# Later first loads, and 16 warming instructions moved ahead, in a recurrence followed by an MLP

## The chip, the cores and the metric

The kernel runs on one core of one Trainium2 chip. The metric is the device time of one execution in microseconds. Engines are named as in the profile: PE (TensorE matmuls), PEld (its weight loads), DVE (VectorE), ACT (ScalarE), POOL (GpSimd), SP (SyncE, which here only issues transfers).

## The reference

The first part is a linear recurrence with a decay for every channel; its output, with the heads side by side, goes through a two-layer MLP with an exact Gelu.

```python
# r, k, v, w: (4, 8, 768, 48) float32; u: (8, 48)
for t in range(S):
    kt, vt, rt, wt = (k[:, :, t], v[:, :, t], r[:, :, t], w[:, :, t])
    cur = np.einsum('bhd,bhe->bhde', u[None] * kt, vt)
    y[:, :, t] = np.einsum('bhd,bhde->bhe', rt, state + cur)
    state = wt[:, :, :, None] * state + np.einsum('bhd,bhe->bhde', kt, vt)
...
x = attn_out.transpose(0, 2, 1, 3).reshape(B * S, H * D)   # 3072 x 384
h = x @ w_in                                               # 384 x 2048
g = 0.5 * h * (1.0 + erf(h * inv_sqrt2))
return g @ w_out                                           # 2048 x 384
```

`w_in` and `w_out` come as float64; the kernel turns them into float32 on the chip.

## The kernel before, in words

The work is cut into eight tiles, x = 0 to 7: a half sequence (T = 384 steps) of one batch element with all eight heads. A tile's recurrence is done in chunks of C = 64 steps. Inside a chunk the decays are gathered by doubling: there are six levels, h = 1, 2, 4, 8, 16, 32. At each level PE makes products of k and r for all chunks (`products`, the matmuls of line 575), DVE copies the part that belongs to this level into `a_sb` under a mask (line 639; at h = 16 and 32 ACT does it, line 636), and DVE multiplies r and k by the decay products of blocks of length h (lines 617 and 628). The level's update needs the level's products to be done, since it overwrites what they read, and the next level's products need the update. At h = 1 there is a second product, the diagonal with u.

The first tile (x = 0) is done in two units of two head pairs each, so that one unit's PE work can lie beside the other's DVE work. After the levels come the transposes of k (line 798), k times v (line 824), the chunk's own y (line 865), the chain of states on DVE (lines 839 and 844), and the states' part of y (line 894). The result is copied to `xT`; the rows of the fourth head pair go there through six small transfers (`pack`, line 886), three issued by SP and three by ACT.

The MLP of tile 0 (`first_mlp`) runs beside the recurrence of tile 1. Its first layer makes one group of 128 hidden units after another (line 1084, three matmuls of the program each, six in the records), in two PSUM banks in turn; the Gelu of line 1086 frees a bank. Later tiles use `mlp`, which lies beside the next tile's recurrence in the same way.

Order on every engine is the order in which the program writes instructions. For each tile a string in `PLAN` sets it: each letter takes the next piece from a stream. In the first tile's string `.` and `s` are the two units, `f` the next tile's recurrence (its first steps), `l` the loads, `c` and `p` the conversion of weights, `w` the next tile's v, and `x` warming matmuls. What is left of the streams after the string is written out behind it.

The transfers around the change are all issued by SP, in order:

- `load_first` (line 274) loads r, k and w of the first tile, in six parts, and behind it `load_v(0, nc.sync)` (line 278) loads v. Neither waits for anything.
- `weight_in(i, True)` (lines 326 and 327) loads the i-th piece of w_in in three thirds of 256 KB. Ahead of each third, DVE writes one element of the destination; the transfer has to wait for that, so the place of the letter `l` in DVE's order paces the transfer.
- `load_second` (lines 285 and 286) loads r, k and w of the second tile in eight shares of 288 KB, paced in the same way.
- Pieces 3 and up come from `conversion` without a mark (line 322).

A piece of weights is converted by three ACT instructions (`prepare`, lines 459, 460 and 462) and two DVE instructions (`finish`, lines 471 and 475). Piece 0 is prepared by the first `c`, piece 1 by the first `p`, piece 2 by the second `p`.

Warming matmuls multiply zeros into a bank that nobody reads (`keep_warm`, line 349). There are 12 of 128 columns at the start, followed by two long ones (line 353); two of 512 columns behind certain `products` of the first tile; and two times three of 512 columns where the string has `x`. On PE each is one weight load and one matmul.

Of the kernel before, what the change touches and what calls it, by code (L numbers as in the profile page):

```python
# [10 lines left out]
F32 = mybir.dt.float32  # L11
# [10 lines left out]
C = 64  # L22
# [10 lines left out]
BANK = 512  # L33
# [3 lines left out]
NC_SP = 8  # L37
HALFWAY = 2
PLAN = {
    0: "l.s....llsl.lssslslss.lc.l.slslls...ssss..lcs.s.s.l.ss..ss..sccs.c.s.llpssslw..cs.ffpccxx",  # L40
    1: (
        "swcs.clc.cs.wccscwcc.csccsw..cwlsccccccsc.cs.swcccc.ccc.s.cwlssccsclcs.cwss.lscccsw.c.cwcw"
        ".s..clw..lw..wwccc..cccc.scc.l.cslfccscfccw.fcffy.w.y..fw....ywyw..yyxxx.wyfxx..x.w..y.fyx"
# [149 lines left out]
def kernel(  # L193
# [9 lines left out]
    nc = tc.nc  # L203
# [12 lines left out]
    io = ctx.enter_context(tc.tile_pool(name="io", bufs=2))  # L216
# [8 lines left out]
    def pair(name):  # L225
        return pools["d"].tile([128, 2, BANK], F32, name=name, tag="d")
# [23 lines left out]
    loaded = {}  # L250

    def units_of(x):
        return NPART if x == 0 else 1
# [4 lines left out]
    bufs = [io.tile([128, 3 * NP * T], F32, name=f"rkw{i}", bufs=1) for i in range(2)]  # L258
# [7 lines left out]
    def load_first():  # L266

        t = bufs[0]
        loaded[0] = [None, None]
        size = 3 * NP * T // units_of(0)  # L270
        nc.scalar.dma_start(out=u_sb, in_=u)
        for i, part in ((0, 2), (0, 0), (0, 1), (1, 0), (1, 1), (1, 2)):
            s = slice(i * size + part * size // 3, i * size + (part + 1) * size // 3)
            nc.sync.dma_start(out=t[:, s], in_=rkw[0, :, s])

    def load_v(x, dma):
        loaded[x][1] = io.tile([128, v.shape[2]], F32, name="v_in", bufs=1)
        dma.dma_start(out=loaded[x][1], in_=v[x])
# [35 lines left out]
    def weight_in(i, gate=False):  # L314

        if i < len(pieces):
            dst, src = pieces[i]
            raws[i] = cv.tile([128, PIECE], I64, name="raw", bufs=AHEAD) if wide else None
            if wide:
                dst = raws[i].rearrange("p (a c) -> p a c", a=dst.shape[1])  # L320
            if not gate:
                nc.sync.dma_start(out=dst, in_=src)
                return
            for a in range(dst.shape[1]):
                if wide:
                    nc.vector.memset(dst[:, a].bitcast(U32)[:, 0:1], 0)
                nc.sync.dma_start(out=dst[:, a], in_=src[:, a])
                yield

    load_first()  # L330
    load_v(0, nc.sync)


    zeros = const.tile([128, BANK], BF16, name="zeros")
# [8 lines left out]
    def keep_warm(n, elsewhere=False, n_cols=BANK):  # L343
        if elsewhere:
            t = pair("warm")[:, 0]
        else:
            t = bank("warm")
        for _ in range(n):
            nc.tensor.matmul(t[:, 0:n_cols], lhsT=zeros[:, 0:128], rhs=zeros[:, 0:n_cols], start=True, stop=True)

    keep_warm(12, n_cols=BANK // 4)
    for _ in range(2):
        nc.tensor.matmul(bank("warm"), lhsT=zeros[:, 0:2 * 128].bitcast(F32), rhs=long_zeros, start=True, stop=True)

# [39 lines left out]
    for i, h in enumerate(QUARTERS[:1]):  # L394
        for a in range(3):
            w_q = (3 - a) * C // 4
            z = q_ints[1 if a == 0 else 2]
# [81 lines left out]
    def attention(x, unit):  # L479
# [3 lines left out]
        np_ = len(parts)  # L483
# [6 lines left out]
        rc, kc = (z.rearrange("p (b i c t) -> p b i c t", b=np_, c=2, t=C) for z in (r, k))  # L490
# [77 lines left out]
        def products(bs, right, width, warm=True):  # L568
            d = pair("d")
            n = 0  # L570
            for b in bs:
                for i in range(NI):
                    for g in range(2):
                        for p in range(2):
                            nc.tensor.matmul(d[half[p], g, n * width:(n + 1) * width],  # L575
                                             lhsT=kc[half[g], b, i, p], rhs=right(half[g], b, i, p),
                                             start=True, stop=True)
                    n += 1
            if x == 0 and warm:
                keep_warm(2)  # L580
            return d[:, :, 0:n * width]
# [10 lines left out]
        def halves():  # L592

            for h in LEVELS:
                m = C // 2 // h
                if np_ < NPART:

                    d = products(range(np_), lambda z, b, i, p: rc[z, b, i, p], C, 1 < h < 8)
                    d = d.rearrange("p g (n m two j) -> p g n m two j", two=2, j=h, m=m)[:, :, :, :, 1, :]
                else:  # L600
                    right = rc.rearrange("p b i c (m two j) -> p b i c m two j", two=2, j=h)[:, :, :, :, :, 1, :]
                    d = products(range(np_), lambda z, b, i, p: right[z, b, i, p], C // 2)
                    d = d.rearrange("p g (n m j) -> p g n m j", j=h, m=m)
                if h == 1:
                    yield
                    diag = diagonal()
                yield

                r2 = r.rearrange("p (n two j) -> p n two j", two=2, j=h)[:, :, 1, :]
                t2 = tot[h].rearrange("p (n two) -> p n two", two=2)[:, :, 0:1].to_broadcast(r2.shape)  # L610
                k2 = k.rearrange("p (n two j) -> p n two j", two=2, j=h)[:, :, 0, :]
                tk = tot[h].rearrange("p (n two) -> p n two", two=2)[:, :, 1:2].to_broadcast(k2.shape)
                rk = bass.AP(tensor=r2.tensor, offset=r2.offset, ap=[r2.ap[0], [n_u - h, 2]] + list(r2.ap[1:]))
                tt = bass.AP(tensor=t2.tensor, offset=t2.offset, ap=[t2.ap[0], [1, 2]] + list(t2.ap[1:]))

                def update(z, r2=r2, t2=t2, k2=k2, tk=tk):
                    nc.vector.tensor_mul(*((k2, k2, tk) if z is k else (r2, r2, t2)))

                if x == 0 and m == 1:

                    update(k)
                    last_r.append(lambda: update(r))
                elif x == 0 and h == 1:
                    update(r)
                    yield
                    update(k)
                else:
                    nc.vector.tensor_mul(rk, rk, tt)
                yield
                ah = at.rearrange("p g n (m two j) -> p g n m two j", two=2, j=h)[:, :, :, :, 1, :]  # L630
                if h >= 16:

                    for p in range(2):
                        for i in range(m):
                            s = slice(p * 64 + i * 2 * h, p * 64 + i * 2 * h + h)
                            nc.scalar.copy(out=ah[s, :, :, i], in_=d[s, :, :, i])
                else:
                    mask = masks[h].rearrange("p (m j) -> p m j", j=h).unsqueeze(1).unsqueeze(1)
                    nc.vector.copy_predicated(out=ah, mask=mask.to_broadcast(ah.shape), data=d)
                if h == 1:  # L640
                    copy_diagonal(diag)
                yield
# [267 lines left out]
        else:  # L910
# [8 lines left out]
            for turn in range(2):  # L919
                for i in range(NI):  # L920
                    for b in range(np_):
                        p = (b + turn) % 2
# [10 lines left out]
            for turn in range(2):  # L933
                ysb = ysb_of() if turn == 0 else ysb
                a = ys[turn][1][:, :, 0:NI * C].rearrange("p b (q i t) -> p b q i t", q=Q, t=C)
                for z in range(2):
                    s = slice(z * G, z * G + D)
# [9 lines left out]
        if split:  # L947
            for c, copy in enumerate((nc.scalar.copy, nc.vector.tensor_copy)):
                for z in range(2):
                    s = slice(z * G, z * G + D)  # L950
                    copy(out=xT[s, 0:Q, :].rearrange("p q (i c t) -> p (q i) c t", c=2, t=C)[:, :, c, :],
                         in_=ys[0][0][c][s, 0:NI * C].rearrange("p (i t) -> p i t", t=C))
# [3 lines left out]
        for b in reversed(range(np_)):  # L956
            for q in reversed(range(Q)):
# [5 lines left out]
                if which < NJ:  # L963
                    for z in range(2):
                        s = slice(z * G, z * G + D)
# [274 lines left out]
    second = load_second(nc.sync)  # L1240
# [13 lines left out]
    def next_v():  # L1254
        load_v(1, nc.sync)
        yield

    def warm():
        for _ in range(2):
            keep_warm(3, True)  # L1260
            yield

    def masks_and_sums():
# [6 lines left out]
    for x in range(NX):  # L1270
        following = attention(x + 1, 0) if x + 1 < NX else iter(())
        if x == 0:
            streams = {
                ".": units[0], "s": units[1], "f": following, "c": pieces_of_w, "w": next_v(), "x": warm(),
                "p": prepare_apart(),
                "l": chain(weight_in(0, True), islice(second, 5), weight_in(1, True), second, weight_in(2, True)),
            }
        else:
            streams = {
                **(mlp(x - 1) if x > 1 else {".": first_mlp()}),  # L1280
                "s": slots, "f": following,
                "l": load(x + 1, nc.sync),
                "x": sums_of_x(x),
                "w": masks_and_sums() if x == 1 else chain(h_sums([1]), o_sums(EARLY, len(FORMS_O))) if x == 2 else iter(()),
                "y": o_sums(0, EARLY) if x == 1 else iter(()),
                "c": pieces_of_w if x == 1 else iter(()),
            }
        for c in PLAN[x]:
            next(streams[c], None)
        for c in ".slxwp" if x == 0 else ".slxwcy" if x == 1 else ".vgeoslxw":  # L1290
            while next(streams[c], streams) is not streams:
                pass
        slots = following
        if x == 1:
            fewer_pairs()
# [63 lines left out]
```

## Time and profile before

| | |
|---|---|
| median of 3 runs | 576.1 us (575.36 to 579.16) |
| profiled execution, its own time | 577.52 us |
| its span, first to last instruction | 575.7 us |
| PE busy | 551.3 us (96%) |
| PEld busy | 491.1 us (85%) |
| DVE busy | 489.2 us (85%) |
| ACT busy | 334.1 us (58%) |
| POOL busy | 106.1 us (18%) |
| granted TensorE clock, mean | 1.00 |

A row in order of time gives the start and the length in us, the engine, the line, the operation, what it writes and reads, how many, and in brackets the idle time before it and what ended that; "issue" stands for a wait that the profile doesn't show. SPq and ACTq are the issuing of transfers. A row of stretches gives the stretch, its length, the busy time of PE, PEld, DVE, ACT and POOL with the number of instructions, the granted clock, the busy share of the 16 DMA engines and GB/s. A row of transfers gives destination and source, the issuing engine, how many, KB each, and the time from issue to landing. Tile names are the program's: `rkw` holds r, k and w, `d` the products, `raw` a weight piece as it is loaded, `v_in` is v.

### The profile page before, as it was taken

The page shows a single profiled execution, that of the slowest core. Times are in us where ns is not written, and L with a number is a line of the kernel's source. Part 1 is how long each engine was busy: PE and PEld are TensorE (multiplying, and loading weights), DVE is VectorE, ACT ScalarE, POOL GpSimd, SP SyncE. Part 2 cuts the span into 40 slices and gives each one's busy share as a digit, 9 for nine tenths or more (in the row PEclk, how much of TensorE's full clock was granted, in tenths as well). Part 3 has the DMA queues.
Part 4 walks back from the last instruction along what each step waited for, and adds up shares of the span by engine and source line. Part 5 has one row for each costly group of instructions (what it writes and reads, how often), then busy time and mean ns, then how long its engine had stood idle before and what let it go on. Part 6 is the DMA issues. An engine that isn't in the chain of part 4 may idle for free. (4 is left out here: it accounts for less than half of the span.)

```text
span 575.7 us, 17712 instructions
## 1 busy us (share of the span) xinstructions
PE 551.3 (96%) x7412; PEld 491.1 (85%) x7420; DVE 489.2 (85%) x977; ACT 334.1 (58%) x768; POOL 106.1 (18%) x105
## 2 busy tenths in 40 slices
PE   7689999999998999999999999999999999999997
PEld 4576665689998989999898998989898988999997
DVE  7889879999989989798989979799888989755464
ACT  2468995347753677347763477527772478535820
POOL 5100000016200460006400252005500072000000
PEclk9999999999999999999999999999999999999999
DMA  8559742239342782558623593337915384200001
GB/s 303 178 159 370 239 142 87 81 86 154 47 82 64 175 106 36 139 156 131 81 46 114 135 165 44 60 91 159 131 30 135 84 105 62 43 25 30 0 1 41
DMA packets 71646, 62.15 MB, mean 108 GB/s; under 512 B 32912, under 2 KB 56720, under 8 KB 71568
## 3 DMA queue, kind: packets, MB, share of 16 engines
q1 hardware_dynamic: 50112, 45.62, 26.4%
q0 software_dynamic: 21216, 15.34, 20.3%
q8 instruction: 58, 0.95, 0.7%
q14 instruction: 20, 0.16, 0.1%
q10 hardware_dynamic: 240, 0.08, 0.1%
HBM read 36.24 MB, written 4.72 MB: 71 GB/s over the span
## 5 line engine op out<-in xcount | busy, mean ns | idle before, releaser
L1148 POOL DMA_DIRECT2D g<-o_sb x78 | 94.9, 1490 | 370.7 <-ACT g L1117 347.2
L1197 DVE TENSOR_TENSOR g<-g 128x512 f32<-128x512 f32 x112 | 75.1, 688 | 24.3 <-PE o_ps L1073 21.3
L1117 ACT COPY o_sb<-u_ps 128x384 f32<-128x384 f32 (+1 forms) x56 | 25.8, 461 | 67.6 <-PE u_ps L1073 66.2
L1073 PE MATMUL h_ps<-forms_x,w_in_sb 128*128 128x192 f32 x280 | 57.7, 332 | 0.0
L1073 PE MATMUL o_ps<-w_out_sb,g 128*128 128x192 f32 x280 | 50.5, 327 | 0.5 <-DVE g L1197 0.5
L1117 ACT COPY g<-h_ps 128x384 f32<-128x384 f32 x84 | 40.4, 482 | 16.3 <-PE h_ps L1073 14.4
L1073 PEld LDWEIGHTS h_ps<-forms_x,w_in_sb 128*128 128x128 f32 x280 | 46.6, 190 | 2.7 <-ACT g L1117 2.2
L1073 PEld LDWEIGHTS o_ps<-w_out_sb,g 128*128 128x128 f32 x280 | 46.0, 190 | 1.2 <-DVE g L1197 0.8
L1166 ACT ACTIVATE g<-g 128x384 f32<-128x384 f32 x98 | 46.2, 519 | 0.3
L1073 PE MATMUL o_ps<-t,g 128*128 128x192 f32 x224 | 41.4, 328 | 0.1
L726 ACT COPY a_sb<-d 32x320 f32<-32x320 f32 (+5 forms) x108 | 39.3, 364 | 3.6 <-DVE a_sb L784 1.7
L1073 PEld LDWEIGHTS o_ps<-t,g 128*128 128x128 f32 x224 | 36.8, 190 | 0.7 <-PE u_ps L1073 0.3
L1073 PE MATMUL h_ps<-forms_x,s 128*128 128x192 f32 x168 | 35.5, 334 | 0.0
L1073 PE MATMUL h_ps<-xT,w_in_sb 128*128 128x192 f32 x168 | 35.0, 331 | 0.1
L710 PE MATMUL d<-kx,rkw 64*64 64x96 f32 x1152 | 32.0, 248 | 3.0 <-ACT a_sb L726 1.9
L710 PEld LDWEIGHTS d<-kx,rkw 64*64 64x64 f32 x1152 | 25.6, 133 | 9.6 <-issue 4.3
L1084 PE MATMUL h_ps<-xT,w_in_sb 128*128 128x384 f32 x96 | 33.0, 494 | 0.2
L1073 PE MATMUL u_ps<-xT,w_in_sb 128*128 128x192 f32 x168 | 32.5, 328 | 0.1
L1073 PE MATMUL u_ps<-w_out_sb,g 128*128 128x192 f32 x168 | 30.9, 332 | 1.4 <-ACT o_sb L1115 0.8
L1092 PE MATMUL o_ps<-w_out_sb,g 128*128 128x384 f32 x96 | 31.7, 489 | 0.0
L575 PEld LDWEIGHTS d<-rkw 64*64 64x64 f32 x1152 | 19.1, 134 | 14.2 <-issue 8.5
L739 DVE COPY_PREDICATED a_sb<-quarter,d 128x480 f32<-128x480 uint8 (+5 forms) x54 | 23.2, 440 | 8.7 <-PE d L710 7.4
(178 smaller groups left out, 1206.2 us busy)
## 6 DMA issues: line engine op xcount, KB each, us to landing
g<-o_sb POOLq DMA_DIRECT2D x78, 192.0 KB, 4.2
rkw<-in_rkw_dram SPq DMA_DIRECT2D x54, 256.0 KB, 3.7
raw<-in_w_out_dram SPq DMA_DIRECT2D x8, 768.0 KB, 5.4
v_in<-in_v_dram SPq DMA_DIRECT2D x8, 584.0 KB, 4.6
out_dram<-o_sb SPq DMA_DIRECT2D x24, 192.0 KB, 2.1
raw<-in_w_in_dram SPq DMA_DIRECT2D x5, 768.0 KB, 9.2
rkw<-kx SPq DMA_DIRECT2D x72, 48.0 KB, 2.1
rkw<-in_rkw_dram SPq DMA_DIRECT2D x6, 384.0 KB, 6.8
```

The costliest lines, as they stand in the source:

```text
L575: nc.tensor.matmul(d[half[p], g, n * width:(n + 1) * width], lhsT=kc[half[g], b, i, p], rhs=right(half[g], b, i, p), start=True, stop=True)
L710: nc.tensor.matmul(d[half[p], g, i * 3 * C // 2:(i + 1) * 3 * C // 2], lhsT=kc[half[g], n // NI, n % NI, p], rhs=rx[half[g], 2 * n + p], s ...
L726: nc.scalar.copy(out=at[z, g, first:behind, (a + 1) * h:], in_=d[z, :, :, to] if g == slice(None) else d[z, :, to])
L739: nc.vector.copy_predicated(out=an[:, :, :, :, (a + 1) * h:], mask=mask.to_broadcast(data.shape), data=data)
L1073: nc.tensor.matmul(o, lhsT=lhsT, rhs=rhs, start=start, stop=True, skip_group_check=True)
L1084: nc.tensor.matmul(h_ps, lhsT=w_in_sb[:, f // FI, j, f % FI * 128:(f % FI + 1) * 128], rhs=xT[:, j, :], start=(j == 0), stop=(j == NJ - 1))
L1092: nc.tensor.matmul(o, lhsT=gs[f // FG][:, f % FG, i * 128:(i + 1) * 128], rhs=w_out_sb[:, f, :], start=(f == 0), stop=(f == NF - 1))
L1117: nc.scalar.copy(out=o, in_=z)
L1148: nc.gpsimd.dma_start(out=o, in_=saved[q, t], accum_op=ALU.add)
L1166: nc.scalar.activation(out=o, in_=z, func=AF.Gelu, scale=MINUS.get(h, 1.0))
L1197: nc.vector.tensor_add(o, o, g_block(what[3:5]))
```

## The change

The order of the first tile's steps other than loads stays the same letter by letter; the `l` letters move, and there are two more of them. Four things are edited:

- v of the first tile is no longer loaded right behind r, k and w. It comes in two halves with marks, as part of the `l` stream, behind the first piece of w_in.
- Every `l` stands later in the string. With the `l` steps written out (`w0` to `w2` the thirds of pieces 0 to 2, `v` the halves of v, `t` the shares of the second tile), the start of the string reads `w0 . s .... w0 w0 s t . t sss t s t ss . t c . w1 . s w1 s w1 t s` before, and `. s .... w0 s . w0 sss w0 s v ss . v c . t . s t ss . t .. t sss t s .. w1` after. Its end reads `w2 w2 p sss w2 w .. c s . ff p cc xx` before, and `t p sss w2 w .. w2 c s . w2 ff p cc xx` after. The `p` ahead of `sss` prepares piece 1, the last one piece 2. The SP part of `pack` is in the third of these `s`.
- The matmuls of the levels h = 2 and h = 4 of both units of the first tile are no longer followed by two warming matmuls each, 8 in all. At the start there are 20 short warming matmuls instead of 12.
- The six warming matmuls at the string's end have 64 columns instead of 512.

```diff
 PLAN = {
-    0: "l.s....llsl.lssslslss.lc.l.slslls...ssss..lcs.s.s.l.ss..ss..sccs.c.s.llpssslw..cs.ffpccxx",
+    0: ".s....ls.lssslslss.lc.l.slss.l..lsssls..lcs.s.sl..lss.l.ss..sccs.lc.s.lpssslw..lcs.lffpccxx",
...
+    def first_v():
+        loaded[0][1] = t = io.tile([128, v.shape[2]], F32, name="v_in", bufs=1)
+        for i in range(2):
+            s = slice(i * v.shape[2] // 2, (i + 1) * v.shape[2] // 2)
+            nc.vector.memset(t[:, s.start:s.start + 1], 0.0)
+            nc.sync.dma_start(out=t[:, s], in_=v[0][:, s])
+            yield
+
     load_first()
-    load_v(0, nc.sync)
...
-    keep_warm(12, n_cols=BANK // 4)
+    keep_warm(20, n_cols=BANK // 4)
...
-                    d = products(range(np_), lambda z, b, i, p: rc[z, b, i, p], C, 1 < h < 8)
+                    d = products(range(np_), lambda z, b, i, p: rc[z, b, i, p], C, False)
...
     def warm():
         for _ in range(2):
-            keep_warm(3, True)
+            keep_warm(3, True, 64)
             yield
...
-                "l": chain(weight_in(0, True), islice(second, 5), weight_in(1, True), second, weight_in(2, True)),
+                "l": chain(weight_in(0, True), first_v(), islice(second, 5), weight_in(1, True), second, weight_in(2, True)),
```

## The prediction

> **What bounds the kernel now.** I read the page first, then the table by stretches, then the order of time of the first 50 us, where the whole edit lies.
>
> ```profile
> span 575.7 us, 17712 instructions
> PE 551.3 (96%) x7412; PEld 491.1 (85%) x7420; DVE 489.2 (85%) x977; ACT 334.1 (58%) x768; POOL 106.1 (18%) x105
> q8 instruction: 58, 0.95, 0.7%
> ```
>
> PE is busy for 96% of the span. The third row is PE's own instructions: 14832 matmuls and weight loads in 58 transfers, so one transfer for every 256 instructions.
>
> ```profile
> 10.00:15.00 5.00, 3.69 (x165) 2.81 (x161) 4.93 (x10) 0.73 (x1) 4.07 (x9) 1.00 0.98 339
> 15.00:20.00 5.00, 3.24 (x127) 2.35 (x121) 4.02 (x10) 2.21 (x3) 2.05 (x3) 1.00 0.70 212
> 40.00:45.00 5.00, 5.00 (x108) 3.41 (x106) 4.83 (x11) 4.82 (x7) 0.00 (x0) 1.00 0.86 263
> 45.00:50.00 5.00, 5.00 (x108) 3.26 (x106) 4.95 (x7) 4.12 (x7) 0.00 (x0) 1.00 1.02 377
> ```
>
> The columns are the length, then PE, PEld, DVE, ACT and POOL busy, the granted clock, the DMA share and GB/s. In the first loop DVE is the fuller engine (4.93 and 4.02 of 5 us against 3.69 and 3.24 of PE). From 40 us on PE has no gap, so whatever the first loop gains or loses at its end is carried to the end of the kernel nearly whole; a wait put into PE at 45 us is carried in the same way.
>
> ```profile
> 13.19 0.80 PE L575 MATMUL d<-rkw 64*64 64x64 f32 x38 [0.24 <-issue]
> 14.46 0.93 PE L575 MATMUL d<-rkw 64*64 64x64 f32 x48
> 15.32 0.39 PE L349 MATMUL warm<-zeros 128*128 128x512 bf16 x1
> 15.86 0.67 PEld L575 LDWEIGHTS d<-rkw 64*64 64x64 f32 x38 [0.42 <-issue]
> 18.12 0.45 PE L575 MATMUL d<-rkw 64*64 64x64 f32 x11 [1.46 <-issue]
> 18.66 0.96 DVE L628 TENSOR_TENSOR rkw<-rkw,tot_sb 128x768 f32<-128x768 f32 x1 [0.45 <-issue]
> 20.03 0.96 DVE L628 TENSOR_TENSOR rkw<-rkw,tot_sb 128x768 f32<-128x768 f32 x1 [0.41 <-PE d L575]
> 22.68 1.39 PE L575 MATMUL d<-rkw 64*64 64x64 f32 x80 [0.61 <-issue]
> 23.43 0.96 DVE L628 TENSOR_TENSOR rkw<-rkw,tot_sb 128x768 f32<-128x768 f32 x1 [0.15 <-PE d L575]
> 26.41 1.49 PEld L575 LDWEIGHTS d<-rkw 64*64 64x64 f32 x95 [0.49 <-issue]
> 27.45 1.20 DVE L617 TENSOR_TENSOR rkw<-rkw,tot_sb 128x384 f32<-128x384 f32 x2 [0.84 <-issue]
> 33.98 0.86 PE L865 MATMUL y_ps<-a_sb,v_in 64*64 64x64 f32 x44 [1.39 <-issue]
> 37.71 1.59 PE L575 MATMUL d<-rkw 64*64 64x32 f32 x94 [0.57 <-issue]
> ```
>
> PE stops in the middle of a burst several times with nothing that releases it. Between the restarts at 13.19 and 18.12 lie 38 pairs of load and matmul, two warming pairs, 48 pairs, two warming pairs and 38 pairs: 128 pairs, 256 instructions. These stops are waits for the next block of instructions, and DVE's idle times at 18.66, 20.03, 23.43 and 27.45 follow bursts that were late through them: 0.45 + 0.41 + 0.15 + 0.84 = 1.85 us. [...]
>
> **The change part by part.** *Eight more short warming matmuls ahead.*
>
> ```profile
> 1.19 1.46 PE L349 MATMUL warm<-zeros 128*128 128x128 bf16 x12 [1.19 <-DVE two L338]
> 2.44 3.73 PE L353 MATMUL warm<-zeros 128*128 128x512 f32 x4
> 6.93 0.93 PE L575 MATMUL d<-rkw 64*64 64x64 f32 x48 [0.76 <-DMA rkw<-in_rkw_dram]
> ```
>
> One costs 1.46 / 12 = 0.12 us, eight cost 0.98. PE waits 0.76 us for the load of k there, so 0.22 us at most comes out the other side, and DVE's first update waits for that burst. Without the cover it would be the whole 0.98.
>
> *Two warming matmuls after each of the second and third levels' four bursts left out.* That is 8 matmuls and 8 weight loads, 16 instructions, the number put in ahead; from the end of the third level every later block boundary falls where it did. In between it falls 16 and then fewer instructions earlier, 16 x 0.93 / 96 = 0.16 us of a burst. A pair costs PE 0.42 us (the idle time of the weight load behind it at 15.86). The four pairs make 1.7 us of PE, but DVE is the fuller engine, so the gain can only come out of its 1.85 us of idle time. A burst that begins 0.42 earlier asks for its next block earlier, and the block itself comes with less traffic around it. The lower bound is no gain, the upper 1.85. The 0.45 and the 0.41 are removed if the third level's bursts move up by the warming pair and half the stop; of the 0.84, 0.49 is a block's wait. I take 1.4 for these, less 0.2 for the start: 1.2 gained. What is late next is DVE itself, which then runs without a gap.
>
> *Six warming matmuls at the loop's end get 64 columns instead of 512.*
>
> ```profile
> 39.24 1.47 PE L349 MATMUL warm<-zeros 128*128 128x512 bf16 x5
> 40.63 1.87 PEld L575 LDWEIGHTS d<-kx,rkw 64*64 64x64 f32 x96 [0.42 <-ACT kx L524]
> ```
>
> The burst behind them waits for ACT's product with u. Nothing is gained; PE now idles there instead.
>
> *The first loads paced.* The first piece of w_in and v are held back by marks that DVE writes between its own operations.
>
> ```profile
> 14.27 0.96 ACT L459 ACTIVATE f<-raw 128x768 f32<-128x768 f32 x1 [4.70 <-DMA raw<-in_w_in_dram]
> 24.18 2.58 ACT L636 COPY a_sb<-d 16x192 f32<-16x192 f32 x8 [6.94 <-PE d L575]
> 29.89 1.03 PE L824 MATMUL kv_ps<-v_in,kx 64*64 64x48 f32 x48 [0.23 <-ACT kx L800]
> ```
>
> ACT idles 6.94 us behind the first piece's conversion, and v, now issued near 15 us, is first read at 29.89. Both delays cost nothing. The marks are 0.06 us of DVE each, one more than before. SP waits at each mark; behind it stand only later loads, and the last mark before the three xT transfers is passed near 31 us, long before these are due.
>
> *The third piece of w_in.* Here the pacing bites. Its three thirds go out one by one; now two leave SP before the xT transfers and one behind them, and after the change all three come behind, with the next tile's v between the first and the second.
>
> ```profile
> 31.20 1.68 SPq L327 DMA_DIRECT2D raw<-in_w_in_dram  x2
> 36.60 1.86 SPq L886 DMA_DIRECT2D xT<-ysb  x3
> 38.57 0.56 SPq L327 DMA_DIRECT2D raw<-in_w_in_dram  x1
> 39.23 1.23 SPq L278 DMA_DIRECT2D v_in<-in_v_dram  x1
> 40.51 0.43 SPq L322 DMA_DIRECT2D raw<-in_w_in_dram  x1
> 42.17 0.93 ACT L459 ACTIVATE f<-raw 128x768 f32<-128x768 f32 x1 [0.15 <-DMA raw<-in_w_in_dram]
> 42.58 6.07 PE L1084 MATMUL h_ps<-xT,w_in_sb 128*128 128x384 f32 x18
> 42.99 1.01 ACT L460 ACTIVATE e<-raw,two 128x768 f32<-128x768 uint32 x1
> 44.03 1.10 ACT L462 ACTIVATE e<-raw 128x768 f16<-128x768 f32 x1
> 45.15 0.49 ACT L1086 ACTIVATE g<-h_ps 128x384 f32<-128x384 f32 x1
> ```
>
> ```profile
> raw<-in_w_in_dram SPq DMA_DIRECT2D x1, 256.0 KB, 3.5
> v_in<-in_v_dram SPq DMA_DIRECT2D x1, 584.0 KB, 5.7
> ```
>
> ACT already waits 0.15 us for this piece now: the third issued at 38.57 takes 3.5. After the change one third takes that place, v follows, and the last two are issued near 40.5 and 41. Ahead of the last byte stand 3 x 256 + 584 KB = 1.38 MB. At 263 GB/s from 40 to 45 us (1.32 MB) and 377 behind that, they are through at 45.2. If v lands as now, at 39.23 + 5.7 = 44.9, the 0.52 MB behind it add 1.4 at 377 GB/s: 46.3, and a little more if pieces behind share. Bounds: 42.17 (no loss, if the rings interleave them ahead of v) and 46.8; I take 46.0, near the end that the v row gives. ACT's conversion then starts 3.83 us later. Behind it in ACT's order stand L460, L462 and the first Gelu; behind that Gelu waits PE, since the first layer has two banks: its third group of six matmuls reuses the bank that the Gelu frees. That group is due at 42.58 + 2/3 x 6.07 = 46.63 and the Gelu now ends at 45.64, a cover of 0.99. PE is stopped 3.83 - 0.99 = 2.84 us; without the cover it would be 3.83. DVE's shift of the same piece waits too, but less than PE. What SP holds behind these thirds is 0.52 MB later, 1.4 us, and is converted behind the late piece anyway.
>
> **The sum.** -1.2 + 2.84 = +1.6 us. The profiled execution took 577.52 us (575.7 of span and 1.8 around it), 1.4 above the median of the runs, 576.1. The changed kernel comes to 579.1 in a like execution and 577.7 in the median. With the bounds: -1.85 (574.3) to +0.22 + 4.63 - 0.99 = +3.9 (580.0); that is the likeliest case's own range.
>
> **The rivals.** *(a) The late piece stays hidden.* Its thirds land by 43 because SP gets through its queue earlier than I count, or the rings let them pass v. For it: the loop itself ends earlier and SP's issues with it. Against it: v's 5.7 us to landing. Then only the gain stands: 576.1 - 1.2 = 574.9.
>
> *(b) The clock falls; slower.* Place: PE's stop ahead of the third group at 46 us, and the second and third levels, where PE was busy 3.24 of 5 us with four of the warming pairs and has less now. Price: at the start the 128-column matmuls take 0.12 us, while 512 columns at 39.24 take 1.47 / 5 = 0.29 or less, so a slow PE is about half as fast, and it stayed so for about 5 us (1.19 to 6.17). Where PE has no gap, 5 us at half speed lose 2.5. In the levels five bursts of 0.93 double, 4.7 us, of which about half hides behind DVE. 577.7 + 2.5 + 2.5 = 582.7. [...]
>
> *(c) The fetch stops vanish.* With light traffic each block comes in time and the bursts close up: 0.24 + 1.46 + 0.61 + 0.49 + 1.39 + 0.57 = 4.8 us of stops and 4 x 0.42 = 1.7 of warming, 6.4 in all: 569.7. Against it: DVE is idle only 1.85 us around them, and the stops at 33.98 and 37.71 lie where the traffic is light already.
>
> *(d) No gain and the latest landing:* 580.0, or a little over it if the pieces behind come late as well.
>
> **How the numbers follow.** The forecast has 0.45, (a) 0.17, (b) 0.24, (c) 0.10, (d) 0.04. One per cent, about what a measurement of this kernel can tell from no change, is 5.8 us: below 570.3 or above 581.9. Faster comes from (c), 0.10; slower from (b) and half of (d), 0.26; the rest, 0.64, is within 1%. The range leaves (c) out below and the upper half of (b) above: 573.8 to 583.0.
>
> **What would show it.** Right: ACT's L459 near 42 to 45 us with several us of idle time that a transfer of raw ended; PE idle ahead of the L1084 matmuls, released by ACT's L1086; DVE's idle times near 18.7 and 20.0 gone; the burst that starts at 36.84 now about 1.2 us earlier; L617's first update up to 0.2 later. Wrong: the conversion without a wait, a granted clock under 1.00 after 10 us, the 1.46 us stop still whole, or a time that moves by over 4 us with the first 50 us as described, which would put the cause behind the first loop.

## The result, and the profile after

The changed kernel took 586.6 us in the median (584.34 to 587.91, six runs) against 578.7 for the kernel before (575.36 to 581.92, six runs beside it): a ratio of 1.0139, 95% interval 1.0096 to 1.0182. It is slower by 1.4%. The forecast was 577.7 with 573.8 to 583.0, 1.6 us more than before; measured were 7.9 us more, so it was wrong. The profiled execution took 586.21 us; before's took 577.52.

The head of the page after:

```profile
span 584.4 us, 17722 instructions
PE 553.5 (95%) x7417; PEld 494.6 (85%) x7420; DVE 490.0 (84%) x979; ACT 333.2 (57%) x768; POOL 106.1 (18%) x105
PEclk9887999999999999999999999999999999999999
```

The span grew by 8.7 us and the engines' sums hardly moved. The last row is the granted clock in 40 slices of 14.6 us: it is below full in slices 2 to 4, so what is lost lies in the first 60 us. The table by stretches of the kernel after (columns as before) says where:

```profile
10.00:15.00 5.00, 3.37 (x176) 2.72 (x167) 4.97 (x9) 0.00 (x0) 4.09 (x9) 1.00 0.46 151
15.00:20.00 5.00, 2.93 (x144) 2.69 (x144) 5.00 (x11) 2.88 (x3) 1.89 (x3) 0.92 0.72 213
30.00:35.00 5.00, 1.88 (x127) 1.74 (x120) 4.34 (x26) 3.25 (x4) 0.00 (x0) 1.00 0.82 262
35.00:40.00 5.00, 4.57 (x140) 4.57 (x143) 1.27 (x5) 0.48 (x1) 0.00 (x0) 0.66 0.03 9
50.00:55.00 5.00, 2.08 (x5) 1.05 (x5) 4.39 (x6) 4.91 (x7) 0.00 (x0) 0.84 1.03 375
```

From 10 to 15 us the loads are thinner (151 GB/s, 339 before), and DVE is full, as foretold. Then PE is busy for only 1.88 us between 30 and 35 and for 2.08 between 50 and 55 (before: 3.61 and 5.00), and with or behind each of these holes stands a granted clock below 1 (0.66 from 35 to 40 us, 0.84 from 50 to 55).

The order of time after, at the places of those holes. First the end of the first loop:

```profile
26.43 0.56 DVE L624 TENSOR_TENSOR rkw<-rkw,tot_sb 128x384 f32<-128x384 f32 x1 [0.66 <-issue]
28.87 0.55 PE L831 MATMUL kv_ps<-v_in,kx 64*64 64x48 f32 x18 [0.23 <-ACT kx L807]
30.18 0.33 SPq L286 DMA_DIRECT2D rkw<-in_rkw_dram  x1
35.43 0.86 PE L872 MATMUL y_ps<-a_sb,v_in 64*64 64x64 f32 x44 [3.55 <-issue]
36.18 3.79 PE L901 MATMUL y_ps<-rkw,st 64*64 64x64 f32 x77
38.45 0.48 ACT L977 COPY ysb<-y_ps 128x384 f32<-128x384 f32 x1 [5.16 <-PE y_ps L901]
```

and the rows of the kernel before for the same steps that the prediction did not show:

```profile
34.73 2.32 PE L894 MATMUL y_ps<-rkw,st 64*64 64x64 f32 x79
36.10 0.48 ACT L970 COPY ysb<-y_ps 128x384 f32<-128x384 f32 x1 [1.79 <-PE y_ps L894]
48.58 1.60 PE L575 MATMUL d<-rkw 64*64 64x32 f32 x96
```

The y burst (44 matmuls of line 872) stops for 3.55 us with nothing that releases it; before the same stop took 1.39. The rows of transfers further down have a packet of the instruction queue (q8) 2.3 us ahead of the restart, at 33.10; the stop is taken from that to be a wait for a block of instructions. The 77 matmuls behind it take 3.79 us, where 79 took 2.32.

Then the MLP's first groups, after:

```profile
40.93 1.31 SPq L327 DMA_DIRECT2D raw<-in_w_in_dram  x1
42.34 0.38 SPq L278 DMA_DIRECT2D v_in<-in_v_dram  x1
42.81 0.86 SPq L327 DMA_DIRECT2D raw<-in_w_in_dram  x2
42.92 2.70 PE L582 MATMUL d<-kx,rkw 64*64 64x64 f32 x96 [1.23 <-ACT kx L531]
45.55 4.61 PE L1091 MATMUL h_ps<-xT,w_in_sb 128*128 128x384 f32 x12
49.64 0.89 ACT L466 ACTIVATE f<-raw 128x768 f32<-128x768 f32 x1 [5.25 <-DMA raw<-in_w_in_dram]
53.09 3.90 PE L1091 MATMUL h_ps<-xT,w_in_sb 128*128 128x384 f32 x6 [2.92 <-ACT g L1093]
56.91 1.60 PE L582 MATMUL d<-rkw 64*64 64x32 f32 x96
```

This is the chain that the prediction drew: two thirds behind v, ACT waiting 5.25 us for `raw`, the Gelu late, PE stopped 2.92 us ahead of the third group. But the six matmuls of that group take 3.90 us, where a group took about 2.0 before (6.07 / 3).

The loss as a running difference, after minus before, at the start of the same event:

| event | before | after | difference |
|---|---|---|---|
| k times v | 29.89 | 28.87 | -1.02 |
| y burst again at work | 33.98 | 35.43 | +1.45 |
| copy of the result (`ysb`) | 36.10 | 38.45 | +2.35 |
| first MLP group | 42.58 | 45.55 | +2.97 |
| third group (before: 42.58 + 2/3 x 6.07) | 46.63 | 53.09 | +6.46 |
| next level's products | 48.58 | 56.91 | +8.33 |
| span | 575.7 | 584.4 | +8.7 |

So the wait for blocks costs 2.47 (2.16 by the longer stop in the y burst, the rest by one of 0.37 in k times v that before did not have), the third piece's stop 2.92, and slower matmuls most of the rest: 0.90 up to the copy, 0.62 up to the first group, 6.46 - 2.97 - 2.92 = 0.57 in the first two groups, and 1.87 in the third. The granted clock of the kernel after is 0.50 in four stretches of 3.41 us each, from 19.24, 36.31, 43.13 and 53.38 us. A table of stretches of 3.4 us shows that the slower matmuls lie where the clock is low:

```profile
32.90:36.30 3.40, 0.87 (x51) 0.87 (x52) 1.91 (x11) 0.39 (x1) 0.00 (x0) 1.00 0.42 156
36.30:39.70 3.40, 3.40 (x78) 3.40 (x75) 0.97 (x5) 0.48 (x1) 0.00 (x0) 0.50 0.02 5
39.70:43.10 3.40, 2.17 (x123) 2.01 (x123) 3.25 (x7) 1.80 (x4) 0.00 (x0) 1.00 0.27 58
43.10:46.50 3.40, 3.40 (x98) 2.98 (x95) 3.26 (x10) 1.28 (x3) 0.00 (x0) 0.51 0.93 320
50.00:53.40 3.40, 0.48 (x2) 0.30 (x2) 2.79 (x3) 3.34 (x5) 0.00 (x0) 1.00 1.05 402
53.40:56.80 3.40, 3.40 (x6) 1.35 (x4) 3.36 (x7) 2.69 (x4) 0.00 (x0) 0.50 0.99 351
```

In these stretches the clock is either 1.00 or 0.50, give or take the rounding of the stretch. Each of the three at half clock follows one that PE did not fill (0.87 us, 2.17, 0.48).

When the late block arrived can be read from the transfers. In the kernel after, between 33.0 and 33.2 us (packets, MB, share of the engines):

```profile
q1 hardware_dynamic: 38, 0.07, 93.5%
q8 instruction: 1, 0.02, 29.8%
```

in the kernel before, between 31.3 and 31.7:

```profile
q8 instruction: 1, 0.02, 18.0%
q1 hardware_dynamic: 10, 0.01, 7.4%
```

Before, the block came some 1.5 us behind the start of k times v, with the rings (the data transfers' queues, q1 in the rows) nearly empty by then (7.4%). After, it came 4.2 us behind it, with the rings still full (93.5%): a 288 KB share of the second tile's loads had been issued at 30.18, on top of an unpaced piece of w_in at 28.68. PE takes up its work some 2.3 to 2.6 us after the block in both (33.10 to 35.43, and 31.36 to 33.98).

### The profile page after: what moved, and what is told of

Read it like the earlier page. It is cut to its first block, busy times and chain, and to the rows that moved or that the text cites. A ratio compares the mean times of both kernels' runs of the same rounds, so it can differ in the third digit from the quotient of the medians.

```text
span 584.4 us, 17722 instructions
## 1 busy us (share of the span) xinstructions
PE 553.5 (95%) x7417; PEld 494.6 (85%) x7420; DVE 490.0 (84%) x979; ACT 333.2 (57%) x768; POOL 106.1 (18%) x105
## 5 line engine op out<-in xcount | busy, mean ns | idle before, releaser
L1091 PE MATMUL h_ps<-xT,w_in_sb 128*128 128x384 f32 x96 | 35.2, 519 | 2.9 <-ACT g L1093 2.9
L1080 PE MATMUL u_ps<-w_out_sb,g 128*128 128x192 f32 x168 | 30.9, 332 | 1.4 <-ACT o_sb L1122 0.8
L1099 PE MATMUL o_ps<-w_out_sb,g 128*128 128x384 f32 x96 | 31.7, 489 | 0.0
L1091 PEld LDWEIGHTS h_ps<-xT,w_in_sb 128*128 128x128 f32 x96 | 18.4, 199 | 15.3 <-ACT g L1093 3.9
```

What stands on the lines that cost most here:

```text
L1080: nc.tensor.matmul(o, lhsT=lhsT, rhs=rhs, start=start, stop=True, skip_group_check=True)
L1091: nc.tensor.matmul(h_ps, lhsT=w_in_sb[:, f // FI, j, f % FI * 128:(f % FI + 1) * 128], rhs=xT[:, j, :], start=(j == 0), stop=(j == NJ - 1))
L1099: nc.tensor.matmul(o, lhsT=gs[f // FG][:, f % FG, i * 128:(i + 1) * 128], rhs=w_out_sb[:, f, :], start=(f == 0), stop=(f == NF - 1))
```

## The experiments

Theory L: the later loads cause the loss, in two places. Traffic on the way when PE asks for its block delays the block, and the third piece of w_in behind v stops PE; behind both stops the clock falls. Theory C: the missing warming matmuls let the clock fall. The kernel before ran beside them at 577.03 us (19 runs; e1 to e4), 577.49 (25 runs; e5 to e8) and 577.26 (23 runs; e9 and e10). Ratios are against it.

### e1: the loads alone

```diff
-    keep_warm(20, n_cols=BANK // 4)
+    keep_warm(12, n_cols=BANK // 4)
-                    d = products(..., C, False)
+                    d = products(..., C, 1 < h < 8)
-            keep_warm(3, True, 64)
+            keep_warm(3, True)
```

> Only the pacing of the loads; all warming matmuls as in the kernel before. Theory C (the missing and shortened warming matmuls let the clock fall, and that is the loss): the loss is gone, within 1.5 us of before, granted clock 1.00 from 7 us to the end. Theory L (the late loads are the loss: a block of instructions that comes late near 33 us, 2.5 us, and the stop of PE ahead of the third group of the first layer, 2.9 us, each with a fall of the clock behind it, 0.9 and 1.9 us): 6 to 9 us slower than before, a stop of over 2 us in the y burst (line of y_ps) and one of over 2 us ahead of the third group, the clock at half only behind these two stops.

Measured: 585.86 us, ratio 1.0149 (1.0096 to 1.0202). From its order of time:

```profile
36.66 1.54 PE L872 MATMUL y_ps<-a_sb,v_in 64*64 64x64 f32 x45 [4.38 <-issue]
55.65 3.88 PE L1091 MATMUL h_ps<-xT,w_in_sb 128*128 128x384 f32 x6 [3.26 <-ACT g L1093]
```

Both stops and the slow third group are there with all warming matmuls in place. Within the intervals the loads alone are the whole loss.

### e2: the warming edits alone

The kernel before with the three edits of `keep_warm` and `products`, its loads and string untouched.

> Only the warming matmuls (20 ahead, none behind the second and third levels, 64 columns at the end); all loads as before. Theory C: 4 to 8 us slower than before, with the clock at half for three or four stretches of 3.4 us. Theory L: between 1.5 us faster and 1.5 us slower than before, no stop of PE over 2 us before 60 us; at most the two falls of the clock that in the changed kernel have no long stop ahead of them (near 19 and 43 us).

Measured: 577.2 us, ratio 0.9997 (0.9959 to 1.0035). Its order of time:

```profile
33.53 0.86 PE L865 MATMUL y_ps<-a_sb,v_in 64*64 64x64 f32 x44 [1.36 <-issue]
42.53 6.07 PE L1084 MATMUL h_ps<-xT,w_in_sb 128*128 128x384 f32 x18
```

The stop is that of before (1.39), the third group has none (18 matmuls in one row), and the first MLP group starts within 0.05 us of before. Theory C is not the loss. This profiled execution had no fall of the clock, but it is not typical: of the ten executions seven have a mean clock of 0.997 or less, against six of nineteen of the kernel before (one stretch of 3.4 us at half clock takes 0.003 off the mean). So without these warming matmuls the clock seems to fall more often (e9 and e10 bear it out), and the time does not show it.

### e3: the thirds of the third piece put back, ahead of v

```diff
-    0: "... .sccs.lc.s.lpssslw..lcs.lffpccxx",
+    0: "... .sccs.lc.s.lllpssslw..cs.ffpccxx",
```

> The changed kernel, with two thirds of the third piece of w_in ahead of the xT transfers again. Theory L: the stop ahead of the third group shrinks from 2.9 us to under 0.5 and the fall of the clock behind it is gone, 4 to 5.5 us faster than the changed kernel (3 to 4.5 slower than before); ACT waits for raw less than 1 us there. Theory C: the stop is not what costs; less than 2 us faster than the changed kernel.

Measured: 581.99 us, ratio 1.0068 (1.0038 to 1.0098).

```profile
26.56 2.23 PE L582 MATMUL d<-rkw 64*64 64x64 f32 x96 [2.13 <-DVE raw L326]
37.09 1.07 PE L872 MATMUL y_ps<-a_sb,v_in 64*64 64x64 f32 x44 [3.25 <-issue]
46.93 6.25 PE L1091 MATMUL h_ps<-xT,w_in_sb 128*128 128x384 f32 x18
```

The stop ahead of the third group is gone and some 4 us with it (a ratio of 1.0068 against 1.0139); the one in the y burst stays, and the kernel is still slower than before. In this execution PE also stopped for 2.13 us at the last level's burst and took 2.23 us over it instead of 1.63 (its mean clock of 0.994 has room for two falls of 3.41 us: one is the granted 0.50 from 37.59 to 41.00, the other is estimated to lie here); before, that stop took 1.03 us, in e1 2.13, in the kernel after 0.87. Without the second place the loss is 0.7% here, with it alone 1.0% (e7), with both 1.4%: near a sum, as far as the intervals tell.

### e4: the end's warming matmuls back to 512 columns

```diff
-            keep_warm(3, True, 64)
+            keep_warm(3, True)
```

> The changed kernel, with 512 columns in the six warming matmuls at the loop's end. Theory C: the fall of the clock near 43 us is gone, the burst of the diagonal with u takes 2.0 us instead of 2.7 and the first two groups of the first layer 4.05 instead of 4.6; if that delay is carried, 1 us faster than the changed kernel. Theory L: the third group's stop is set by the landing of the third piece, so the time at which that group starts stays the same and less than 0.7 us is gained.

Measured: 585.96 us, ratio 1.0149 (1.0101 to 1.0196): nothing is won. The fall near 43 us is gone (granted clock 1.00 from 43.99 to 57.60), as theory C has it, and the first two groups take 4.14 us instead of 4.61; but the third group starts at 52.70 against 53.09, as theory L has it, since the late piece decides. The third group and two stretches:

```profile
52.70 2.20 PE L1091 MATMUL h_ps<-xT,w_in_sb 128*128 128x384 f32 x6 [3.65 <-ACT g L1093]
```

```profile
47.40:50.81 3.41, 1.64 (x6) 0.63 (x4) 0.83 (x3) 1.55 (x2) 0.00 (x0) 1.00 1.01 369
50.81:54.23 3.42, 1.53 (x5) 1.00 (x6) 3.39 (x3) 3.36 (x5) 0.00 (x0) 1.00 1.04 393
```

In this execution the stop is longer than in the kernel after (3.65 against 2.92), and yet the third group runs at full clock (1.00 from 50.81 to 57.60). Here the stop lies across two stretches, with PE busy for 1.64 and 1.53 us in them; in the kernel after it filled one (0.48). So the length of the stop alone did not decide here; that it is how the stop falls into the stretches is the author's estimate from these two executions.

### e5 and e8: the loads caught up earlier

In e5 the same steps in another order, so that all shares of the second tile are issued ahead of the y burst and the thirds stand where they stood before; e8 is e5 with the end's warming matmuls at 512 columns.

```diff
-    0: ".s....ls.lssslslss.lc.l.slss.l..lsssls..lcs.s.sl..lss.l.ss..sccs.lc.s.lpssslw..lcs.lffpccxx",
+    0: ".s....lsl.lsssslss.lc.ll.llsllss.ll..ssssll..lcs.s.s..ss..ss..sccs.c.s.llpssslw..cs.ffpccxx",
```

> The changed kernel, with the first 20 us of its pacing kept and all shares of the second tile and the second piece of w_in issued by 25 us, the third piece's first two thirds ahead of the xT transfers. Theory L (two places: transfers between 28 and 35 us hold up PE's next block of instructions, and the third piece lands late): the stop in the y burst falls from 3.5 to under 1.6 us, the third group starts by 47 us, and the time is between 1 us faster and 1 us slower than before. Theory C (the shortened warming): still over 2 us slower than before.

> As the caught-up kernel, with 512 columns in the six warming matmuls at the loop's end. Theory L: no difference over 1 us from the caught-up kernel. Theory C, with the falls near 43 us: 0.5 to 1.5 us faster than it and fewer executions with a mean clock under 1.00.

Measured: 580.81 us, 1.0054 (1.0028 to 1.008), and 580.79, 1.0057 (1.0023 to 1.0091). From the order of time of e5, then of e8:

```profile
28.30 2.84 PE L582 MATMUL d<-rkw 64*64 64x64 f32 x96 [3.77 <-issue]
36.95 0.86 PE L872 MATMUL y_ps<-a_sb,v_in 64*64 64x64 f32 x44 [0.64 <-issue]
```

```profile
27.48 2.84 PE L582 MATMUL d<-rkw 64*64 64x64 f32 x96 [2.96 <-issue]
```

The y burst's stop fell to 0.64 us, as theory L has it, but hardly any time was won over e3 (1.0054 against 1.0068): the last shares and piece 3 now go out between 22.70 and 24.41 (e5), and at the last level's burst, which took 1.63 us before behind a stop of 1.03, PE stops for 3.77 us and then takes 2.84 over it. By theory L the traffic now lies on an earlier block; no run shows when that block came. The mean clock of both executions is 0.994, which has room for two falls of 3.41 us; that the slow burst lies in one is an estimate from that. The time was expected within 1 us of before's; it is about 3 us slower. The wide warming matmuls of e8 change nothing.

### e6: e3, and the unpaced piece of w_in issued later

```diff
-        for _ in weight_in(i + 3):
-            pass
+        if i:
+            for _ in weight_in(i + 3):
+                pass
...                                   # behind the next tile's v:
+        for _ in weight_in(3):
+            pass
```

> The kernel with two thirds of the third piece ahead of the xT transfers, and besides piece 3 (768 KB, the one without marks) issued only behind the next tile's v, so that between 28 and 35 us only two shares of the second tile are on their way. Theory L, with the block of instructions held up by what is queued: the block near the y burst starts by 32 us instead of 34.8, the stop there falls from 3.3 to under 2 us, and the copy of y is at least 1.5 us earlier; piece 3 now lands some 2 us late for ACT, so the whole is only 0 to 3 us faster than with the thirds alone. If the block is late for another reason (the clock, the queue of PE), the stop stays over 2.8 us.

Measured: 578.6 us, ratio 1.0021 (0.9995 to 1.0047), against e3's 1.0068.

```profile
30.02 0.62 PE L832 MATMUL kv_ps<-v_in,kx 64*64 64x48 f32 x28 [1.19 <-issue]
34.57 1.29 PE L873 MATMUL y_ps<-a_sb,v_in 64*64 64x64 f32 x45 [2.46 <-issue]
45.13 6.07 PE L1092 MATMUL h_ps<-xT,w_in_sb 128*128 128x384 f32 x18
```

With 768 KB less issued ahead of the block, the y burst's stop is 2.46 us instead of 3.25, between the two marks of the expectation (under 2, over 2.8); the last share and two thirds, issued from 29.6 to 30.9, are still ahead of it. By itself this is no proof of the first place. K times v, one block earlier, now stops for 1.19 us, where e3 has no stop, so the two stops together are 3.65 us. And the two traces lie 2.87 us apart at k times v already (28.28 against 31.15), by a delay that begins at 26.56 in e3, before piece 3 is issued there. What fits theory L is the time that the block takes: from the restart of k times v to the next block's packet 2.3 us (30.02 to 32.30), in the kernel after 3.3 (29.78 to 33.10).

All twelve traces together bear the first place out better. In the five in which the last share of the second tile is issued behind the start of k times v (after, e1, e3, e4, e6), the y burst stops for 2.46 to 4.38 us; in the seven others the stop is 0.64 to 1.39. Where a run shows the block's packet, it comes 3.7 to 4.8 us behind that start in the first set (after, e1, e3, e6) and 1.5 to 2.0 in the second (before, e2, e7). To the seven belong e5 and e8, which differ from the kernel after and from e4 in nothing but the places of the loads. That the block waits because the loads stand ahead of it in the queues is inferred from this; the block was not delayed by itself in any run.

### e7: the kernel before, with its thirds alone moved to the places of after

```diff
-    0: "... ..sccs.c.s.llpssslw..cs.ffpccxx",
+    0: "... ..sccs.c.s.pssslw..lcs.lffpccxx",
```

> The kernel before, with nothing changed but the places of the third piece's thirds (one ahead of and two behind the next tile's v, all behind the xT transfers). By the prediction's own term: ACT's conversion starts 3.8 us later, PE stops 2.8 us ahead of the third group, 2.8 us slower than before. With the clock falling behind the stop, as in the changed kernel: 2.8 plus 1.7, 3.5 to 5.5 us slower. The y burst's stop stays at 1.4 us.

Measured: 583.67 us, ratio 1.0101 (1.0054 to 1.0148).

```profile
28.49 0.91 PE L824 MATMUL kv_ps<-v_in,kx 64*64 64x48 f32 x48 [0.23 <-ACT kx L800]
45.84 0.89 ACT L459 ACTIVATE f<-raw 128x768 f32<-128x768 f32 x1 [5.46 <-DMA raw<-in_w_in_dram]
49.27 4.21 PE L1084 MATMUL h_ps<-xT,w_in_sb 128*128 128x384 f32 x6 [4.19 <-ACT g L1086]
53.41 2.21 PE L575 MATMUL d<-rkw 64*64 64x32 f32 x96
```

The second place by itself costs about 6 us: a stop of 4.19, then half clock (0.50 granted from 47.97 to 54.80) for the third group (4.21 instead of about 2.0) and the products behind it (2.21 instead of 1.60). The stop is longer than the 2.92 of the kernel after, since ACT starts on the late piece 4.90 us behind the first MLP group here (45.84 - 40.94), there 4.09, and the first two groups take 4.14 us here, there 4.61.

This run shows one more thing. Up to k times v its program is that of before, and yet that step came at 28.49 us, 1.40 earlier. Differences of that size in the first loop lie within what single executions differ by.

### e9 and e10: the thirds between the steps behind k times v

e9 is the kernel before, e10 is e2, both with

```diff
-    0: "... ..sccs.c.s.llpssslw..cs.ffpccxx",
+    0: "... ..sccs.c.s.pslslslw..cs.ffpccxx",
```

> The kernel before, with the three thirds of the third w_in piece put between the steps that follow the first tile's k times v (end of the string `p s l s l s l w .. cs . ff`), so that they are neither on the way when PE asks for its block at the y burst nor behind the next tile's v. Theory L (queued loads delay the block; a third piece behind v stops PE): the first loop is as early as in e7_thirds_moved (k times v near 28.5 us, first MLP group near 41.0 us instead of 42.58), the thirds are issued near 33 to 36 us, the conversion waits under 0.5 us, all 18 matmuls of the first layer run without a stop; 1 to 2 us faster than before, and no clock fall behind 30 us. Rival (any third behind the y burst costs a stop): the conversion waits 2 us or more and the third group is stopped 1 us or more; the time is equal to before or up to 3 us slower.

> The same place of the thirds, with the warming edits of the change (20 short matmuls ahead, none at the second and third level, 64 columns at the string's end). Theory L with the warming edits worth what e2_warm_only showed (0.7 us at k times v, nothing at the end): first MLP group at 40.3 to 41.0 us, time within 1 us of e9_thirds_between. Rival theory C (the missing warming matmuls let the clock fall): a granted clock under 1.00 for one window of 3.4 us behind 15 us, and 1.5 us or more slower than e9_thirds_between.

Measured: e9 578.63 us, ratio 1.0017 (0.9998 to 1.0037); e10 579.62, ratio 1.0035 (1.0003 to 1.0067). From the order of time of e9, then of e10:

```profile
32.99 0.86 PE L865 MATMUL y_ps<-a_sb,v_in 64*64 64x64 f32 x44 [1.13 <-issue]
37.55 1.60 PE L575 MATMUL d<-rkw 64*64 64x32 f32 x94 [1.17 <-issue]
42.01 1.27 PE L575 MATMUL d<-kx,rkw 64*64 64x64 f32 x69 [0.86 <-issue]
```

```profile
41.73 6.07 PE L1084 MATMUL h_ps<-xT,w_in_sb 128*128 128x384 f32 x18
```

and a stretch of e10:

```profile
18.40:21.80 3.40, 2.73 (x97) 2.41 (x91) 3.13 (x5) 0.00 (x0) 0.00 (x0) 0.66 0.88 288
```

The hoped-for gain of 1 to 2 us is missed, though no stop is left in the first layer's 18 matmuls. In e9 the y burst's stop is 0.26 us shorter than before's, but the next blocks come later (1.17 against 0.57, and 0.86 where before had none). In e10 the MLP starts 0.85 us earlier than before, in a span of 576.1 us against 575.7, so that gain is given back behind it. e10's profiled clock is 0.997 and e9's 1.000: e10 has one fall in the second and third levels (0.84 granted from 15.00 to 18.40, 0.66 from 18.40 to 21.80), where its warming matmuls are missing, as theory C has it. It is no chance of one execution: 11 of e10's 12 have a mean clock of 0.997 or less, of e9's 12 five. Whether the one us between the medians is its price is not settled. No version beat the kernel before.

## Why the prediction was wrong, point by point

- **The paced first loads "cost nothing": the step that failed.** The prediction looked only at who reads these loads (the conversion's 6.94 us of idle time, v first read at 29.89) and wrote of the next block that it comes "with less traffic around it". The traffic was less only up to 15 us (151 against 339 GB/s). Pacing did not remove the traffic here, it moved it (262 against 191 GB/s from 30 to 35 us): the shares of the second tile, formerly issued before 27 us, now end at 30.18, just ahead of the block that PE needs in the y burst (its packet at 33.10). The stop there grew from 1.39 to 3.55 us (e1: 4.38). A term put at nothing cost 2.47 us, and 0.9 more by the low clock behind it. The prediction had quoted that stop, and set it aside as lying "where the traffic is light already"; it didn't ask what the traffic there would be after the change.
- **The clock was a rival and belonged in the sum.** Its place, PE's stop at 46 us, and its price, half speed, were right (0.50 granted from 53.38, behind the stop of 2.92). The time that it gave, 582.7, is the nearest of all cases, in part by luck: 2.5 us of it are for the second and third levels, and it lacks the y burst. Its 5 us at half speed were an estimate from the matmuls at the start, beside which before's granted clock is 1.00 (0 to 6.5 us); the falls measured took 3.41 us (after, four of them, and e1 from 55.66) or twice that (6.83: e1 from 35.17, e7 from 47.97). It was given 0.24; before's stop of 1.46 us at 18.12 had kept a granted clock of 1.00. The forecast's own stop was 2.84: behind stops of 2.92, 3.26 and 4.19 us the clock fell, behind one of 3.65 it did not (e4). The falls cost 0.90 + 0.62 + 0.57 + 1.87 = 4.0 us here; the 0.62 and 0.57 are the fall near 43 us, which e4's wide warming matmuls took away without a gain in time. In the second and third levels, the rival's other place, there was a fall too (0.92 granted from 15 to 20 us); at most it is in the 0.38 us by which DVE's wait for the next burst grew (0.15 to 0.53 at 22.58). The falls did not need a PE without work: a stretch of 3.4 us with 0.87 us of PE work was followed by half clock, and so was one with 2.17, while 1.64 and 1.53 us in e4 kept full clock. What the clock goes by, no run shows.
- **The third piece, 2.84 us: right.** Measured 2.92, by the chain as drawn (ACT's L466 waits for `raw`, the Gelu of L1093 releases PE). Both parts of the working were larger, and cancelled: ACT started 4.1 us after the first MLP group (49.64 - 45.55) where the forecast had 3.83 - 0.41 = 3.4, and the first two groups took 4.61 instead of 4.05. On its own (e7) the stop is 4.19: the piece's landing hangs on SP's order, the due time on how early the loop ends, and the forecast's cover of 0.99 held for one loop end only.
- **The first loop's gain, 1.2 us: not decided.** k times v came 1.02 us earlier. DVE's idle times of 0.45 and 0.41 went away, as listed, but that of 0.15 grew to 0.53 and that of 0.84 only fell to 0.66: of the 1.85 us, 1.19 are left, a gain of 0.66 where the forecast had 1.4. Another 0.6 was there from the start, as the first products, which wait for k, began at 6.30 instead of 6.93, and some 0.3 was lost again between. The products began that early in e7 too (6.31), whose start is that of before; the 0.2 us of delay taken for the start did not show. In any case e7 and e9, which have before's program up to k times v, came there 1.40 and 0.72 us earlier too. By its ratio, e2 bounds what the warming edits bring to between 2.4 us gained and 2.0 lost.
- **The rivals.** That the late piece stays hidden and that the fetch stops vanish are both out. A rival was missing: that later loads make a block of instructions later.
- **The range** ended at 583.0, near rival (b), which counts one long stop of PE. There were two, each with a fall behind it, and the second alone (e7, ratio 1.0101) would take 576.1 to 581.9.

## What to carry to other kernels

Pacing a load moves its traffic to where something else is due, and PE's own instruction blocks are among the things that are due (here one came 4.2 us behind the start of k times v instead of 1.5): for every unexplained stop of PE, look at which transfers are on the way then and which will be after the change. A PE stop should be counted once with a half-speed stretch behind it and once without: here the stops of 3.55, 2.92 (after) and 4.19 us (e7) had one that cost 0.9, 1.9 and 2.8 us on top, and the one of 3.65 (e4) had none. And in this kernel, whose loads just fit, moving a stop by reordering loads mostly moved it to another place (e5: 0.64 us in the y burst and 3.77 at the last level; e8: 0.88 and 2.96; e9: 1.13, and 1.17 and 0.86 behind it); where 768 KB were taken out of the stage (e6), the stop got shorter and the one at the block before longer.

## What was not expected of the hardware

- The same block of PE's instructions came about 1.5 us behind the start of k times v with the rings 7% busy and 4.2 us behind it with the rings 93% busy. The block is a single packet of 0.02 MB, yet it came 3.7 to 4.8 us behind in four runs in which loads had just been queued (after, e1, e3, e6). The share at its arrival alone does not give the delay: in e7 it came 1.5 us behind with the rings 54% busy.
- Issuing one transfer on SP took 1.23 us before (39.23), 1.31 after (40.93) and 1.78 in e7 (36.92), against 0.38 for the v load at 42.34. In the first two a block of instructions began to come within 0.4 us of that start (38.90, 40.92); whether that is the cause was not tried.
- What keeps the granted clock at 1.00 stays open. By the stretches of 3.4 us that the runs show, it fell to 0.50 behind 0.20 us (e1), 0.48 (after), 0.50 (e3), 0.53 (e7), 0.54 (e1) and 0.87 (after), and also behind 1.72 and 2.17 (after, up to 19.24 and 43.1); behind 1.53 and 1.64 (e4) it stayed at 1.00.
